# Attention, mish MoE and Sinkhorn experts: row sums turned as they are, and the sign of early weights made on GpSimd

## Chip, cores and metric

One Trainium2 chip, one core. The metric is the device time of one execution in microseconds (us); lower is better. A span is the time from the first to the last instruction of the program in a profiled execution.

## What is computed

```python
def _attn_ref(q, k, v):
    B, H, S, D = q.shape                       # 2, 8, 1152, 64
    q_pool = q.reshape(B, H, S // 2, 2, D).mean(axis=3)
    scores = 1.0 / np.sqrt(D) * np.matmul(q_pool, k.transpose(0, 1, 3, 2))
    scores = scores - np.max(scores, axis=-1, keepdims=True)
    attn = np.exp(scores)
    attn = attn / (np.sum(attn, axis=-1, keepdims=True) + 1e-09)
    return np.matmul(attn, v)
```

The heads are joined to x (1152 x 512). Then follow a mish feed-forward, `(h * tanh(softplus(h))) @ w_out` with `h = x @ w_in` (512 to 2048 to 512), and eight relu experts (512 to 1024 to 512) whose outputs are summed with weights from a gate that eight Sinkhorn rounds normalize. `w_in` and `w_out` arrive as 64-bit floats, all else as 32-bit.

## The kernel before

Every matmul works on a high and a low half of each operand, so that three products stand for one of full precision. The stages follow one another: attention (to about 265 us), mish (to about 480), the experts (to the end).

**Attention.** Heads are worked in eight pairs, each with nine query tiles of 128 rows: step g = 9p + t is tile t of pair p. Step g issues the scores of tile g and their eviction from PSUM with the row minimum (`scores`, line 483, tile e), the transposes of tile g - 3 with their split into eth (ScalarE, line 563) and etl (VectorE, line 566), the DMA that copies e to er for the transposes (`hand_over`, line 503, on SyncE's queue), products with v whose evictions write xs (line 598), and the exponentials with row sums (`exps`, line 497). The transposes and all small turns share four PSUM buffers (tag "t"). A PSUM buffer is free again when its last reader is done.

**The row sums.** `exps` collects the sums of a pair in rs (128 x 9). In the next pair, at t = 0, `row_sums` (lines 505 to 508) adds epsilon and takes the reciprocal on VectorE. At t = 1 `turn_sums` (510 to 528) transposes rs on TensorE into the PSUM tile psr (9 x 128), VectorE copies it to rt (line 515), and two DMAs on SyncE's queue follow: at the start of the next step `out` writes rt to the DRAM tile row (line 520), and at the start of the step behind it `back` reads row into rx in three broadcasts (line 526). SyncE works its queue in order: an er copy that is issued behind one of these waits with it. GpSimd multiplies xs by rx some steps later (line 607).

**The weights.** `load_w` plans the loading of 64-bit weights with a time for each step (`plan64`, lines 136 to 192): a load of the raw tile, a scaling of the high word on GpSimd or ScalarE, a scaling of the low word on ScalarE, a shift by three bits with a mask (`shift`), the sign bit put back (`sign`), an integer add on GpSimd (`join`), and the split into halves. The planner keeps a list for each engine, and each step runs what is due. Tiles with `busy=True` are worked during attention: the four tiles of the first w_in group (due at steps 16, 25, 34 and 43) and two of w_out (52 and 60). For them the shift and the sign are cut in two halves of 128 x 256; the shift of the first half is due two steps after the scaling, the sign of the first half one step later, then the second shift and sign. For a tile due at step 16 these are steps 18 to 21, so t = 0 to 3 of pair 2. `mask` is a constant column that the shift of these tiles reads as its second tensor. The tile of tag "wt" that they write has two buffers.

Of the kernel before, what the change touches and what calls it, by code (L numbers as in the profile page):

```python
# [8 lines left out]
F32 = mybir.dt.float32  # L9
# [3 lines left out]
U32 = mybir.dt.uint32  # L13
AF = mybir.ActivationFunctionType
ALU = mybir.AluOpType
# [8 lines left out]
def pool_attention_mish_sinkhorn_kernel(  # L24
# [12 lines left out]
    nc = tc.nc  # L37
    P = 128
# [10 lines left out]
    QTL = 2 * SQ // P  # L49
# [5 lines left out]
    GF = 512  # L55
    NFC = GF // P
    EPS = 1e-9

    const = ctx.enter_context(tc.tile_pool(name="const", bufs=1))
# [6 lines left out]
    make_identity(nc, ident)  # L66
    identr = const.tile([P, P], F32R, name="identr")
    nc.vector.tensor_copy(identr, ident)
    mask = const.tile([P, 1], U32, name="mask")
    nc.vector.memset(mask, 0x7FFFFFF8)  # L70
    ones = const.tile([P, P], F32, name="ones")
    nc.vector.memset(ones, 1.0)

# [26 lines left out]
    wpools = {0: wa}  # L100
# [3 lines left out]
    def at(t, eng, f):  # L104
        queue[eng].append((t, f))
# [12 lines left out]
    def load_w(which, i, times, stage, late="pool", parts=1, busy=False):  # L118
# [17 lines left out]
        def plan64(u, t):  # L136
            box = {}

            def dma():
                raw = wraw.tile([P, 2 * GF], F32, tag="raw", name=f"raw{which}_{i}_{u}")  # L140
                nc.sync.dma_start(out=raw.bitcast(I64), in_=src[:, u, :])
                w = raw.rearrange("p (n two) -> p n two", two=2)
                box["l"], box["h"] = w[:, :, 0], w[:, :, 1]

            def scale(x):
                if x and busy:
                    nc.gpsimd.tensor_scalar(box["h"], box["h"], 2.0 ** -112, 0.0, op0=ALU.mult, op1=ALU.add)
                elif x:  # L150
                    nc.scalar.activation(box["h"], box["h"], AF.Copy, scale=2.0 ** -112)
                else:
                    nc.scalar.activation(box["l"].bitcast(I32), box["l"].bitcast(U32), AF.Copy, scale=2.0 ** -29)

            def shift(cs=slice(0, GF)):
                if "t" not in box:
                    box["t"] = wpools["t"].tile([P, GF], U32, tag="wt", name=f"wt{which}_{i}_{u}")
                h = box["h"][:, cs].bitcast(U32)
                if busy:
                    nc.vector.scalar_tensor_tensor(  # L160
                        out=box["t"][:, cs], in0=h, scalar=3, in1=mask.to_broadcast(list(h.shape)),
                        op0=ALU.logical_shift_left, op1=ALU.bitwise_and)
                else:
                    nc.vector.tensor_scalar(
                        box["t"][:, cs], h, 3, 0x7FFFFFF8, op0=ALU.logical_shift_left, op1=ALU.bitwise_and)

            def sign(cs=slice(0, GF)):
                t = box["t"][:, cs]
                nc.vector.scalar_tensor_tensor(  # L169
                    out=t, in0=box["h"][:, cs].bitcast(U32), scalar=0x80000000, in1=t,  # L170
                    op0=ALU.bitwise_and, op1=ALU.bitwise_or)

            def join():
                t = box["t"].bitcast(I32)
                nc.gpsimd.tensor_tensor(out=t, in0=t, in1=box["l"].bitcast(I32), op=ALU.add)  # L175

            ts = t if isinstance(t, tuple) else [t + j * stage for j in range(5)]
            at(ts[0] - 2.4 * stage, "dma", dma)
            at(ts[0], "pool" if busy else "act", lambda: scale(1))
            at(ts[0] + parts - 1, "act", lambda: scale(0))  # L180
            for j in range(parts):
                cs = slice(j * GF // parts, (j + 1) * GF // parts)
                at(ts[1] + 2 * j, "dve", lambda cs=cs: shift(cs))
                at(ts[1] + 2 * j + parts - 1, "dve", lambda cs=cs: sign(cs))
            at(ts[2], "pool", join)
            if busy and late == "pool":
                at(ts[3], "pool", lambda: hi(nc.gpsimd, u, box["t"].bitcast(F32)))
            else:
                at(ts[3], "act", lambda: hi(nc.scalar, u, box["t"].bitcast(F32)))
            at(ts[4], late, lambda: lo(u, box["t"].bitcast(F32)))  # L190
# [107 lines left out]
    with ExitStack() as actx:  # L298
# [25 lines left out]
        tiny = pool("tiny", 4)  # L324
        wpools["t"] = pool("wt", 2)

        eps = tiny.tile([P, 1], F32, tag="eps", name="eps", bufs=1)
        nc.vector.memset(eps, EPS)
        qz = []
        for i in range(2):  # L330
            t = z_p.tile([P, 2, 2, P], F32R, name=f"qz{i}")
# [134 lines left out]
        scS, eS, erS, rsS, rxS = {}, {}, {}, {}, {}  # L466
# [35 lines left out]
            er = erS[g] = er_p.tile([P, S], F32R, tag="er", name=f"er{g}")  # L502
            nc.sync.dma_start(out=er.bitcast(F32), in_=e)

        def row_sums(p):
            rs = rsS[p]
            nc.vector.tensor_tensor(out=rs, in0=rs, in1=eps.to_broadcast([P, QTL]), op=ALU.add)
            nc.vector.reciprocal(rs, rs)

        def turn_sums(p):  # L510

            ps = ps_t.tile([P, 4, P], F32, tag="t", name=f"psr{p}")
            nc.tensor.transpose(ps[0:QTL, 0, :], rsS.pop(p), ident)
            rt = rx_p.tile([QTL, P], F32, tag="rt", name=f"rt{p}")
            nc.vector.tensor_copy(rt, ps[0:QTL, 0, :])
            row = row_p.tile([QTL, P], F32, tag="row", name=f"row{p}")
            rx = rxS[p] = rx_p.tile([P, SQ], F32, tag="rx", name=f"rx{p}")

# [196 lines left out]
        for g in range(T0 + EARLY):  # L715
            p, t = divmod(g, QTL)
# [16 lines left out]
            else:  # L733
# [19 lines left out]
                    f()  # L753
                if g < NQ:
                    exps(g)
            if p and t == 0:
                row_sums(p - 1)
            if p and t == 1:
                turn_sums(p - 1)
            if late:  # L760
# [573 lines left out]
```

## Time and profile before

| | |
|---|---|
| median of 3 runs | 1220.34 us (1220.3 to 1220.45) |
| the profiled execution | 1223.26 us |
| its span | 1221.5 us |
| TensorE (PE) busy | 1203.7 us, 99% |
| VectorE (DVE) busy | 855.8 us, 70% |
| GpSimd (POOL) busy | 654.0 us, 54% |
| ScalarE (ACT) busy | 592.1 us, 48% |
| granted TensorE clock | full throughout |

Busy time is the union of an engine's instructions. TensorE's instructions are pipelined, and its busy time holds some waiting. Busy shares over the whole span mix stages that are limited by different engines, so views of single stretches are needed. The waits view names who waited for whom, by the event that came last. The timeline shows single instructions in order.

### The profile page before, as it was taken

The page shows a single profiled execution, that of the slowest core. Times are in us where ns is not written, and L with a number is a line of the kernel's source. Part 1 is how long each engine was busy: PE and PEld are TensorE (multiplying, and loading weights), DVE is VectorE, ACT ScalarE, POOL GpSimd, SP SyncE. Part 2 cuts the span into 40 slices and gives each one's busy share as a digit, 9 for nine tenths or more (in the row PEclk, how much of TensorE's full clock was granted, in tenths as well). Part 3 has the DMA queues.
Part 4 walks back from the last instruction along what each step waited for, and adds up shares of the span by engine and source line. Part 5 has one row for each costly group of instructions (what it writes and reads, how often), then busy time and mean ns, then how long its engine had stood idle before and what let it go on. Part 6 is the DMA issues. An engine that isn't in the chain of part 4 may idle for free.

```text
span 1221.5 us, 19362 instructions
## 1 busy us (share of the span) xinstructions
PE 1203.7 (99%) x6840; PEld 1110.4 (91%) x6840; DVE 855.8 (70%) x1598; ACT 592.1 (48%) x1354; POOL 654.0 (54%) x752
## 2 busy tenths in 40 slices
PE   8899999999999999999999999999999999999998
PEld 8899999999999999898888889999888889999887
DVE  7899999876444333787866677766866777866865
ACT  7888889877544443543332233333333233333331
POOL 7667777415444331485755566555555565555551
PEclk9999999999999999999999999999999999999999
DMA  6787787653223210011111111111011111111112
GB/s 202 265 281 263 272 264 255 232 179 120 88 71 98 74 31 30 1 52 53 32 38 45 52 48 49 52 52 52 23 40 52 53 44 52 53 52 38 37 39 78
DMA packets 51985, 116.39 MB, mean 95 GB/s; under 512 B 7977, under 2 KB 22897, under 8 KB 51889
## 3 DMA queue, kind: packets, MB, share of 16 engines
q1 hardware_dynamic: 48400, 103.36, 25.9%
q0 software_dynamic: 3488, 11.80, 3.3%
q8 instruction: 54, 0.88, 0.3%
q14 instruction: 43, 0.34, 0.1%
HBM read 66.86 MB, written 2.40 MB: 57 GB/s over the span
## 4 chain that ended last, share of the span: by engine, by line
PE 90%; DVE 5%; DMA 4%; ACT 1%; issue 1%; POOL 0%; POOLq 0%; ACTq 0%
PE po L1237 30%; PE c L1067 26%; PE ph L231 10%; PE po L806 8%; PE psS L478 4%; PE psA L581 4%; DMA er<-e 4%; PE psT L560 3%; DVE e L483 2%; DVE etl L566 1%; PE psk L410 1%; PE psw L646 0%; ACT eth L563 0%; PE pg L861 0%; PE psq L456 0%
## 5 line engine op out<-in xcount | busy, mean ns | idle before, releaser
L83 POOL TENSOR_TENSOR wslotsl<-s,wslotsh 128x256 fp32r<-128x256 f32 x180 | 132.0, 743 | 237.1 <-ACT wslotsh L76 237.1
L1245 DVE SCALAR_TENSOR_TENSOR oacc<-po,Pm,oacc 128x512 f32<-128x512 f32 (+1 forms) x217 | 161.1, 746 | 102.2 <-PE po L1237 95.8
L1237 PE MATMUL po<-wdbl,hhall 128*128 128x512 f32 (+1 forms) x543 | 214.4, 395 | 0.0
L1237 PE MATMUL po<-wdbh,hlall 128*128 128x512 f32 (+1 forms) x543 | 214.1, 394 | 0.0
L1237 PE MATMUL po<-wdbh,hhall 128*128 128x512 f32 (+1 forms) x543 | 214.0, 394 | 0.0
L1084 ACT ACTIVATE t<-c 128x384 f32<-128x384 f32 x80 | 39.3, 491 | 246.2 <-PE c L1067 246.2
L1104 ACT ACTIVATE hhall<-c 128x384 fp32r<-128x384 f32 x180 | 88.6, 492 | 127.4 <-DVE c L1100 124.7
L1237 PEld LDWEIGHTS po<-wdbh,hhall 128*128 128x128 f32 x543 | 102.1, 188 | 24.3
L1237 PEld LDWEIGHTS po<-wdbl,hhall 128*128 128x128 f32 x543 | 102.1, 188 | 23.3
L1237 PEld LDWEIGHTS po<-wdbh,hlall 128*128 128x128 f32 x543 | 102.1, 188 | 23.2
L83 POOL TENSOR_TENSOR wslotsl<-rawu,wslotsh 128x256 fp32r<-128x256 f32 x120 | 90.9, 772 | 49.8 <-ACT wslotsh L76 49.8
L483 DVE TENSOR_SCALAR_CACHE_REDUCE e<-psS 128x1152 f32<-128x1152 f32 x72 | 97.3, 1352 | 22.0 <-PE psS L478 11.7
L566 DVE TENSOR_TENSOR etl<-psT,eth 128x384 fp32r<-128x384 f32 (+1 forms) x240 | 108.0, 507 | 4.8 <-ACT eth L563 4.2
L563 ACT ACTIVATE eth<-psT 128x384 fp32r<-128x384 f32 (+1 forms) x240 | 92.8, 477 | 15.6 <-PE psT L560 15.2
L1105 DVE SCALAR_TENSOR_TENSOR hlall<-c,hhall 128x384 fp32r<-128x384 f32 x180 | 98.7, 548 | 2.1
L1067 PE MATMUL c<-x2l,wslotsh 128*128 128x384 f32 x280 | 94.3, 337 | 0.0
L1067 PE MATMUL c<-x2h,wslotsl 128*128 128x384 f32 x280 | 94.1, 336 | 0.0
L1067 PE MATMUL c<-x2h,wslotsh 128*128 128x384 f32 x280 | 93.8, 335 | 0.0
L497 ACT ACTIVATE e<-e,nm 128x1152 f32<-128x1152 f32 x70 | 89.3, 1276 | 0.1
L175 POOL TENSOR_TENSOR wt<-wt,raw 128x512 int32<-128x512 int32 x32 | 42.4, 1325 | 84.0 <-DVE wt L169 59.8
L478 PE MATMUL psS<-kT,qT 128*128 128x384 f32 x384 | 81.9, 348 | 2.8 <-DVE e L483 2.7
L76 ACT ACTIVATE wslotsh<-s 128x256 fp32r<-128x256 f32 x180 | 72.0, 411 | 24.3 <-DVE s L1033 24.3
(365 smaller groups left out, 3117.2 us busy)
## 6 DMA issues: line engine op xcount, KB each, us to landing
er<-e SPq DMA_DIRECT2D x70, 576.0 KB, 4.1
rawd<-in_moe_w_dram SPq DMA_DIRECT2D x60, 256.0 KB, 2.7
rawu<-in_moe_w_dram SPq DMA_DIRECT2D x30, 384.0 KB, 3.3
raw<-in_moe_w_in_dram SPq DMA_DIRECT2D x16, 512.0 KB, 4.3
raw<-in_moe_w_out_dram SPq DMA_DIRECT2D x16, 512.0 KB, 3.7
vraw<-in_v_dram POOLq DMA_DIRECT2D x15, 288.0 KB, 4.7
kraw<-in_k_dram POOLq DMA_DIRECT2D x13, 288.0 KB, 4.6
qT<-qT SPq DMA_DIRECT2D x28, 128.0 KB, 3.1
```

Of the source, the lines that this page charges most:

```text
L83: eng.tensor_tensor(out=lo, in0=src, in1=hi.bitcast(F32), op=ALU.subtract)
L231: nc.tensor.matmul(ps[:, 0:TH], lhsT=a, rhs=b, start=(n == 0), stop=(n == len(ops) - 1))
L478: nc.tensor.matmul(ps[:, kb, 0:TH], lhsT=a, rhs=kt[:, kb * TH:(kb + 1) * TH], start=(n == 0), stop=(n == len(ops) - 1))
L483: nc.vector.tensor_scalar(sc, ps[:, :, 0:TH], -1.0, None, op0=ALU.mult, op1=ALU.min, accum_out=nm)
L497: nc.scalar.activation(e, sc, AF.Exp, bias=nm, scale=-1.0, accum_out=rsS[p][:, t:t + 1])
L563: nc.scalar.activation(eh[:, cs, o:o + b - a], ps[:, 0:3, a:b], AF.Copy)
L566: nc.vector.tensor_tensor(out=el[:, cs, o:o + b - a], in0=ps[:, 0:3, a:b], in1=eh[:, cs, o:o + b - a].bitcast(F32), op=ALU.subtract)
L806: nc.tensor.matmul(ps[:, 0:TH], lhsT=a, rhs=b, start=(n == 0), stop=(n == len(ops) - 1))
L1067: nc.tensor.matmul(cb[c], lhsT=a_, rhs=b_, start=FIRST[n] and m == 0, stop=LAST[n] and m == len(ops) - 1, skip_group_check=True)
L1105: los.append(lambda: nc.vector.scalar_tensor_tensor(out=lo, in0=b, scalar=0.0, in1=hi.bitcast(F32), op0=ALU.max, op1=ALU.subtract))
L1237: nc.tensor.matmul(ps[:, 0:w], lhsT=a, rhs=b[:, cs], start=(n == 0), stop=(n == len(ops) - 1))
L1245: nc.vector.scalar_tensor_tensor(out=oa, in0=ps[:, 0:w], scalar=gate, in1=oa, op0=ALU.mult, op1=ALU.add)
```

## The change

The constant `mask` and the tile `eps` go. `row_sums` goes: rs is transposed as `exps` left it, and in `turn_sums` VectorE adds epsilon in place in PSUM and writes the reciprocal of the 9 x 128 block to rt. For the tiles with `busy=True` GpSimd multiplies the high word twice by 2^-112 into the tile of tag "wt" (which is taken at that moment and no longer at the shift): what is left is a zero with the sign of the weight. The shift then joins its result with that zero by an or where it masked before, and `sign` isn't planned for these tiles any more.

```diff
-    mask = const.tile([P, 1], U32, name="mask")
-    nc.vector.memset(mask, 0x7FFFFFF8)
...
             def scale(x):
                 if x and busy:
+                    box["t"] = wpools["t"].tile([P, GF], U32, tag="wt", name=f"wt{which}_{i}_{u}")
+                    nc.gpsimd.tensor_scalar(
+                        box["t"].bitcast(F32), box["h"], 2.0 ** -112, 2.0 ** -112, op0=ALU.mult, op1=ALU.mult)
                     nc.gpsimd.tensor_scalar(box["h"], box["h"], 2.0 ** -112, 0.0, op0=ALU.mult, op1=ALU.add)
...
                 if busy:
                     nc.vector.scalar_tensor_tensor(
-                        out=box["t"][:, cs], in0=h, scalar=3, in1=mask.to_broadcast(list(h.shape)),
-                        op0=ALU.logical_shift_left, op1=ALU.bitwise_and)
+                        out=box["t"][:, cs], in0=h, scalar=3, in1=box["t"][:, cs],
+                        op0=ALU.logical_shift_left, op1=ALU.bitwise_or)
...
                 at(ts[1] + 2 * j, "dve", lambda cs=cs: shift(cs))
-                at(ts[1] + 2 * j + parts - 1, "dve", lambda cs=cs: sign(cs))
+                if not busy:
+                    at(ts[1] + 2 * j + parts - 1, "dve", lambda cs=cs: sign(cs))
...
-        eps = tiny.tile([P, 1], F32, tag="eps", name="eps", bufs=1)
-        nc.vector.memset(eps, EPS)
...
-        def row_sums(p):
-            rs = rsS[p]
-            nc.vector.tensor_tensor(out=rs, in0=rs, in1=eps.to_broadcast([P, QTL]), op=ALU.add)
-            nc.vector.reciprocal(rs, rs)
-
         def turn_sums(p):
 
             ps = ps_t.tile([P, 4, P], F32, tag="t", name=f"psr{p}")
             nc.tensor.transpose(ps[0:QTL, 0, :], rsS.pop(p), ident)
             rt = rx_p.tile([QTL, P], F32, tag="rt", name=f"rt{p}")
-            nc.vector.tensor_copy(rt, ps[0:QTL, 0, :])
+            sums = ps[0:QTL, 0, :]
+            nc.vector.tensor_scalar(sums, sums, EPS, None, op0=ALU.add)
+            nc.vector.reciprocal(rt, sums)
...
-            if p and t == 0:
-                row_sums(p - 1)
             if p and t == 1:
                 turn_sums(p - 1)
```

## Rows read from the trace of the kernel before

**Rows 1.** The page, busy time, share and instructions of each engine.
```profile
PE 1203.7 (99%) x6840; PEld 1110.4 (91%) x6840; DVE 855.8 (70%) x1598; ACT 592.1 (48%) x1354; POOL 654.0 (54%) x752
```

**Rows 2.** Windows of pair 3: PE, PEld, DVE, ACT, POOL busy, clock, DMA.
```profile
100.71:112.15 11.44, 11.43 (x94) 11.06 (x92) 11.34 (x25) 10.34 (x25) 9.84 (x13) 1.00 0.81 265
...
120.00:130.00 10.00, 9.54 (x80) 9.20 (x80) 8.61 (x18) 9.29 (x24) 9.44 (x10) 1.00 0.63 233
```

**Rows 3.** Waits, whole span, and SyncE's queue: us in total, times, longest.
```profile
PE psT L560 <- DMA er<-e: 7.6, 8, 2.0
...
SPq L526 <- DMA row<-rt: 11.5, 8, 2.5
```

**Rows 4.** Timeline of VectorE, pair 3, steps 0 and 1: start us, length us.
```profile
102.00 0.72 DVE L160 SCALAR_TENSOR_TENSOR wt<-raw,mask 128x256 uint32<-128x256 uint32 x1
...
104.44 0.15 DVE L507 TENSOR_TENSOR rs<-rs,eps 128x9 f32<-128x9 f32 x1
104.62 0.21 DVE L508 RECIPROCAL rs<-rs 128x9 f32<-128x9 f32 x1
104.75 1.33 DVE L483 TENSOR_SCALAR_CACHE_REDUCE e<-psS 128x1152 f32<-128x1152 f32 x1
...
106.00 0.94 DVE L169 SCALAR_TENSOR_TENSOR wt<-raw,wt 128x256 uint32<-128x256 uint32 x1
106.87 1.47 DVE L566 TENSOR_TENSOR etl<-psT,eth 128x384 fp32r<-128x384 f32 x3
108.26 0.27 DVE L515 COPY rt<-psr 9x128 f32<-9x128 f32 x1
```

**Rows 5.** Timeline of SyncE's queue, pair 3: start us, issue time us.
```profile
108.56 0.30 SPq L520 DMA_DIRECT2D row<-rt  x1
109.16 0.48 SPq L503 DMA_DIRECT2D er<-e  x1
112.02 1.75 SPq L526 DMA_DIRECT2D rx<-row  x3
113.88 0.53 SPq L503 DMA_DIRECT2D er<-e  x1
```

**Rows 6.** Timelines of ScalarE and TensorE, pair 3: two single pieces.
```profile
105.54 1.26 ACT L563 ACTIVATE eth<-psT 128x384 fp32r<-128x384 f32 x3
...
116.40 0.93 PE L560 MATMUL psT<-identr,er 128*128 128x128 f32 x9 [0.45 <-DMA er<-e]
```

**Rows 7.** Windows of line 169 alone, step 1 of pairs 2, 4, 5, 6.
```profile
74.00:76.00 2.00, 1.26 (x1) 1.00 0.61 217
...
138.00:140.00 2.00, 1.25 (x1) 1.00 0.88 323
170.00:171.00 1.00, 0.42 (x1) 1.00 1.00 371
202.00:204.00 2.00, 0.90 (x1) 1.00 0.16 46
```

**Rows 8.** Single lines: duration ns min/median/max, first and last start us, forms.
```profile
L507 DVE TENSOR_TENSOR rs<-rs,eps x8: 147/150/592, 39.9 to 261.8; 128x9 f32<-128x9 f32 x8
...
L508 DVE RECIPROCAL rs<-rs x8: 215/216/218, 40.1 to 262.0; 128x9 f32<-128x9 f32 x8
...
L900 DVE RECIPROCAL crec<-psk x8: 191/198/208, 522.7 to 562.9; 128x8 f32<-128x8 f32 x8
...
L149 POOL TENSOR_SCALAR raw<-raw x6: 639/659/680, 61.2 to 220.7; 128x512 f32<-128x512 f32 x6
```

**Rows 9.** Timeline of GpSimd, pair 3, steps 0 and 1.
```profile
101.01 1.42 POOL L83 TENSOR_TENSOR vst<-vraw,vst 128x576 fp32r<-128x576 f32 x1
...
104.57 0.68 POOL L80 TENSOR_SCALAR qst<-qraw 128x576 fp32r<-128x576 f32 x1 [0.54 <-PE psq L456]
```

**Rows 10.** Timelines of VectorE and TensorE, pair 1, steps 1 and 2.
```profile
43.39 0.27 DVE L515 COPY rt<-psr 9x128 f32<-9x128 f32 x1
...
43.78 0.93 PE L560 MATMUL psT<-identr,er 128*128 128x128 f32 x9
```

## The prediction

> **What bounds the kernel now.** I read the page first: TensorE is busy for 99% of the span [rows 1], so a change off TensorE counts only where TensorE is held up. The edits all lie in the attention stage, so the next view is the busy time by windows: in pair 3's first three steps (100.71 to 112.15 us) VectorE is busy for 11.34 of 11.44 us, more tightly packed than ScalarE or GpSimd; later in the same pair (120 to 130 us) it is busy for 8.61 of 10 [rows 2]. VectorE therefore has no room in steps t = 0 to 2 of a pair and some after that. The waits name what TensorE then pays for: 7.6 us in eight waits of the transposes for the copy er<-e, and on the DMA-issuing queue of SyncE 11.5 us in eight waits for the row write row<-rt [rows 3]. The two belong together, which the timelines of pair 3 show. VectorE finishes rt at 108.53 [rows 4]; SyncE issues the row write at 108.56, one er copy at 109.16, and then stands until the row has landed; the three rx reads go out at 112.02, and only behind them the next er copy, at 113.88 [rows 5]. TensorE's transposes at 116.40 waited 0.45 us for such a copy [rows 6]. So the end of rt is a point on the path: what makes it later makes the er copies, and with them TensorE, later.
>
> **The change, part by part, on pair 3.** The loop turns the sums of the pair before at steps t = 0 and 1 of pairs 1 to 7, and once in the tail.
>
> Removed at t = 0: the add of epsilon (0.15) and the reciprocal over 9 columns (0.21). From the add's start at 104.44 to the next eviction at 104.75 that is 0.31 us of VectorE's queue [rows 4]. Removed at t = 1: one half of the sign work, 0.94 us in pair 3, 0.87 from its start to that of the first etl (106.00 to 106.87) [rows 4]; in pairs 2, 4, 5 and 6 it took 1.26, 1.25, 0.42 and 0.90 [rows 7]. The undisturbed time is the 0.42 of pair 5; the rest is waiting for GpSimd, see below. The other half, at t = 3, goes too, but it stands behind that step's eviction, where VectorE has room: I count it as nothing, and if that room were gone it would give back up to 0.42 a pair. Pairs 1 and the tail have no sign work; in pair 7 it falls at t = 0 and 2.
>
> How much of this reaches rt? The three etl subtractions need eth from ScalarE. The first eth started at 105.54, the three take 1.26 overlapped, so one takes about 0.5 (estimate) and the first was ready near 106.04; the first etl started at 106.87 [rows 4, 6]. So etl can come forward by at most about 0.8, however much VectorE is freed.
>
> Added at t = 1, in place of the copy rt<-psr (0.27, 9 rows by 128 columns): an add of epsilon in PSUM and a reciprocal from PSUM, both over 128 columns. The add I price as the copy, 0.27, of the same shape from the same place; between it and the reciprocal stands a semaphore of VectorE on itself (the old pair had 0.03 between its add's end at 104.59 and its reciprocal at 104.62 [rows 4]). The reciprocal over 128 columns is not in the trace. Nearest rows: 9 columns from SBUF take 0.216, against 0.150 for the add over the same 9; 8 columns from PSUM take 0.198 [rows 8]. If the surplus is a fixed price, 128 columns take (0.216 - 0.150) + 0.27 = 0.34. If it is a price per column, the surplus of 0.066 over 9 columns is 7.3 ns each, and 0.27 + 128 x 0.0073 = 1.21. Bounds 0.34 and 1.21. I take 1.2: one column more costs 18 ns between the two reciprocals, though they read different memories, and a fixed surplus leaves no reason for such a step. A gain at this place is excluded: an add of the copy's shape stands where the copy stood, and the reciprocal comes on top.
> The Trainium skill, "VectorE: DVE Perf Modes", section "First, the fixed hardware budget", says that the reciprocal is an iterative division with a repeat count of 8. No run here shows the 128 columns; as eight cycles a column of the page's 0.96 GHz that would be 1.07 us besides the fixed part (an estimate from that page), so the sum would be that of the upper bound, and it speaks against turning the sums before dividing: the same 1152 quotients lie 9 in a row before and 128 in a row after.
>
> So rt and the next eviction move by 0.27 + 0.03 + 1.2 - 0.27 = +1.24, less what etl comes forward.
>
> GpSimd: six times a second TENSOR_SCALAR, priced by the old one at 0.66 (128x512) [rows 8], 3.9 us in all. It stands ahead of the scaling of the same tile, two tiles of buffer being enough, and ahead of the k and v splits queued behind it. In pair 3 the queue runs without a gap into the vst subtraction at 101.01 to 102.43 [rows 9]. The shift that stays on VectorE reads two SBUF tensors, as before; it started at 102.00, took 0.72 and ended 0.29 behind that subtraction, where the undisturbed one ends 0.42 behind its own start [rows 4, 9]. A GpSimd queue that is 0.66 later keeps it up to 0.65 longer: that cost is my estimate for pairs 3 to 6, with nothing as the other end (pair 2's shift lies behind the subtraction). Behind it GpSimd waits 0.54 us for TensorE's psq at 104.57 [rows 9], which takes up most of the 0.66; beyond the shift I cost it at nothing, and without that wait it would be 0.66 on the k and q splits.
>
> Forward move of etl, so: pair 3: 0.31 + 0.87 - 0.65 = 0.53. Pairs 2 and 4, with 1.26 and 1.25: more than 0.8, so 0.8. Pair 5: 0.31 + 0.35 - 0.65, plus 0.44 as its old add took 0.59 instead of 0.15 [rows 8], = 0.45. Pair 6: 0.31 + 0.83 - 0.65 = 0.49. Net on rt: +0.44, +0.71, +0.44, +0.79, +0.75 for pairs 2 to 6, 3.1 us together. All are on the path by the reading above: the er copies queue behind the row write.
>
> Pairs 1 and 7 have little or no sign work at t = 1, so rt is later by most of 1.24, where VectorE has room at t = 3. There the cost comes by another way: psr lies in one of four PSUM buffers of the transposes, the third group of the next step takes the same buffer, and it is free only when rt is written. In pair 1 rt was done at 43.66 and that step's nine transposes ran 43.78 to 44.71, the third group from about 44.4 [rows 10]; rt at 44.90 holds TensorE for 0.5. I take 0.45 for each of the two, with 0 and 1.24 as the ends. In the tail the turned sums feed only GpSimd's scaling; TensorE has other matmuls by then: nothing.
>
> Sum: 3.1 + 0.9 = 4.0 us. The profiled execution took 1223.26 with a span of 1221.5; the median is 1220.34, and the difference is applied to that: 1224.3.
>
> **Rivals.** (a) The reciprocal has a fixed price, 0.34. Then rt moves by 0.27 + 0.03 + 0.34 - 0.27 = +0.37 less the forward moves: -0.43, -0.16, -0.43, -0.08, -0.12 in pairs 2 to 6, and nothing in 1 and 7: 1220.34 - 1.2 = 1219.1, not slower. It decides at a reciprocal under about 0.8 us. For it: no row has more than 9 columns. Against it: the 18 ns for one more column.
> (b) The later rt is hidden: the er copies are held by their buffers (the transposes of two steps before), not by the row write, and the PSUM buffer is free in time; 1220.3 to 1222.3. For it: er copies wait for transposes too. Against it: SyncE's er copy leaves 0.6 behind the row write and the next one right behind the rx reads [rows 5].
> (c) The forward move is worth nothing, as ScalarE's eth is pushed back with TensorE: 7 x 1.24 = 8.7, so 1229.0. For it: eth hangs on transposes that wait for VectorE. Against it: VectorE's freed time lies ahead of the added time in each pair.
> (d) The saving goes through whole and the price is (a)'s: pairs 2 to 6 free 1.50, 1.18, 1.49, 1.10 and 1.14 if GpSimd does not disturb the shift, 6.4 less 5 x 0.37: 1215.8. It needs both the cheap reciprocal and an eth that comes forward too.
>
> **How the numbers follow.** Forecast 0.57 (own range 1222.9 to 1227.0, from GpSimd's part at nothing to pairs 1 and 7 at their upper end), (a) 0.08, (b) 0.20, (c) 0.10, (d) 0.05. A measurement of this kernel can tell about 0.2%, 2.4 us, from no change. Slower: nearly all of the forecast, and (c): 0.64. Same: (a), (b) and the forecast's lower edge: 0.30. Faster: (d) and a part of (a): 0.06. The range 1219.0 to 1228.0 leaves out (d), most of (c) and little else.
>
> **What would show it.** The reciprocal at 1.1 to 1.25 us for 9x128; no add and reciprocal at t = 0; the sign rows gone from the attention stage; two GpSimd rows of 0.66 per early weight tile; the row write 0.4 to 0.8 later after the eviction of step t = 1; the waits of TensorE for er<-e longer than 7.6 us, and new ones of the transposes for VectorE's rt; the mish and expert stages the same to 0.1%. A reciprocal under 0.8, or the er waits unchanged, makes it wrong.

## The result and the profile after

The changed kernel takes 1226.38 us in the median (1225.58 to 1228.59), the kernel before, beside it, 1220.32 (1218.06 to 1220.45): a ratio of 1.0057 with a 95% interval of 1.0039 to 1.0075, some 7.0 us slower. The forecast was 1224.3, slower, with a range from 1219.0 to 1228.0.

The granted TensorE clock is full (1.00, 2.4 GHz) in the profiled executions of before and after. In some of those below it was 0.50 (1.2 GHz) for a stretch of 3.4 us: with the sign alone from 59.1 us, after TensorE had been busy for 2.3 of the 4.1 us ahead of it, with the multiplications alone from 210.2, after 2.6 of 4.2. In three sets of runs the kernel before took 2.3 to 4.9 us longer, in the median, at a mean clock of 0.998 than at 1.000.

The profiled execution took 1225.82 us. Its page, the span and the busy time of each engine, answers to [rows 1]:

```profile
span 1223.9 us, 19355 instructions
PE 1208.4 (99%) x6840; PEld 1114.5 (91%) x6840; DVE 858.0 (70%) x1576; ACT 592.1 (48%) x1354; POOL 656.4 (54%) x758
```

VectorE has 22 instructions fewer and 2.2 us more of work; GpSimd has six more and 2.4 us more. The 22 are eight on the row sums (24 gone, 16 come), twelve sign halves and the fills of two constants. TensorE's busy time grew by 4.7 us though it has the same 6840 instructions. That is the first sign of something that the prediction had not looked at.

The waits, us in total, times, longest; TensorE, then SyncE's queue, answering to [rows 3]:

```profile
PE psT L557 <- DMA er<-e: 2.8, 4, 1.0
PE psS L478 <- DVE e L483: 2.7, 4, 1.5
PE psT L557 <- DVE etl L563: 1.0, 2, 0.7
PE psq L456 <- DVE etl L563: 0.8, 2, 0.4
...
SPq L523 <- DMA row<-rt: 10.5, 7, 2.4
```

The waits for er<-e did not grow from 7.6 us, they fell to 2.8. The profiled execution of before took 1223.26, 2.9 us over the median, and its waits of this kind stand at the top of what all kernels below show (1.7 to 7.6), so this pair of profiles can't settle what attention lost. In what follows medians decide on attention, and the trace only shows how.

VectorE's timeline in pair 3, steps 0 and 1 (start us, length us), answering to [rows 4]:

```profile
102.01 0.47 DVE L595 TENSOR_TENSOR xs<-psA,avt 64x320 f32<-64x320 f32 x1
102.41 1.34 DVE L483 TENSOR_SCALAR_CACHE_REDUCE e<-psS 128x1152 f32<-128x1152 f32 x1
103.68 0.07 DVE L483 DVE_READ_ACCUMULATOR e<-psS 128x1 f32 x1
103.99 1.49 DVE L563 TENSOR_TENSOR etl<-psT,eth 128x384 fp32r<-128x384 f32 x3 [0.23 <-ACT eth L560]
105.39 0.28 DVE L511 TENSOR_SCALAR psr<-psr 9x128 f32<-9x128 f32 x1
105.70 0.94 DVE L512 RECIPROCAL rt<-psr 9x128 f32<-9x128 f32 x1
106.58 1.28 DVE L483 TENSOR_SCALAR_CACHE_REDUCE e<-psS 128x1152 f32<-128x1152 f32 x1
```

Nothing stands between xs and the eviction any more, and nothing between the eviction and etl, which now waits 0.23 us for ScalarE's eth. The add and the reciprocal over 128 columns stand where the copy stood. Single lines of the changed kernel (ns min/median/max, first and last start us):

```profile
L511 DVE TENSOR_SCALAR psr<-psr x8: 277/277/277, 41.3 to 264.1; 9x128 f32<-9x128 f32 x8
L512 DVE RECIPROCAL rt<-psr x8: 945/946/947, 41.6 to 264.4; 9x128 f32<-9x128 f32 x8
L161 DVE SCALAR_TENSOR_TENSOR wt<-raw,wt x12: 407/586/2086, 67.6 to 232.2; 128x256 uint32<-128x256 uint32 x12
L150 POOL TENSOR_SCALAR raw<-raw x6: 645/664/687, 61.0 to 220.7; 128x512 f32<-128x512 f32 x6
```

The reciprocal takes 0.946 us, the new multiplication on GpSimd as long as the old one. And one half of the shift, 0.41 us by itself, took up to 2.09.

**The stages.** Lines of matmuls by their tiles carry the first and the last start, so they give the lengths of the stages. ph begins mish, c begins the experts, the last po ends them. First the kernel before (ns min/median/max; first and last start us):

```profile
L231 PE MATMUL ph<-xh,wul x192: 334/336/420, 264.8 to 442.5; 128*128 128x384 f32 x192
L806 PE MATMUL po<-hhall,wdl x144: 334/336/338, 276.1 to 470.8; 128*128 128x384 f32 x144
L1067 PE MATMUL c<-x2h,wslotsl x280: 331/334/424, 524.1 to 1196.4; 128*128 128x384 f32 x140
L1237 PE MATMUL po<-wdbh,hhall x543: 276/393/398, 540.6 to 1217.7; 128*128 128x512 f32 x179, 128*128 128x256 f32 x2
```

Then the changed kernel:

```profile
L233 PE MATMUL ph<-xh,wul x192: 334/336/420, 263.0 to 442.6; 128*128 128x384 f32 x192
L801 PE MATMUL po<-hhall,wdl x144: 334/340/341, 274.4 to 471.2; 128*128 128x384 f32 x144
L1062 PE MATMUL c<-x2h,wslotsl x280: 334/336/424, 524.5 to 1198.7; 128*128 128x384 f32 x140
L1232 PE MATMUL po<-wdbh,hhall x543: 276/395/397, 541.0 to 1220.1; 128*128 128x512 f32 x179, 128*128 128x256 f32 x2
```

Before, mish takes 524.1 - 264.8 = 259.3 us and the experts 1217.7 - 524.1 = 693.6. After, 261.5 and 695.6. No instruction of either stage was touched, the granted clock is full in both, and yet they are 2.2 and 2.0 us longer. The median matmul of one line is 340 ns long in place of 336, that of another 336 in place of 334. From one start to the next, the 144 matmuls po<-hhall,wdl are 176.5 ns apart on average, before 173.4; most others of 384 columns moved by up to 3 ns, some by nothing. This is 4.2 of the 7.0 us.

### The profile page after: what moved, and what is told of

It is laid out like the page before. It is cut to its first block, busy times and chain, and to the rows that moved or that the text cites. A ratio compares the mean times of both kernels' runs of the same rounds, so it can differ in the third digit from the quotient of the medians.

```text
span 1223.9 us, 19355 instructions
## 1 busy us (share of the span) xinstructions
PE 1208.4 (99%) x6840; PEld 1114.5 (91%) x6840; DVE 858.0 (70%) x1576; ACT 592.1 (48%) x1354; POOL 656.4 (54%) x758
## 4 chain that ended last, share of the span: by engine, by line
PE 94%; DVE 2%; DMA 2%; ACT 1%; issue 1%; SPq 0%; POOL 0%; POOLq 0%; ACTq 0%
PE po L1232 30%; PE c L1062 26%; PE ph L233 10%; PE po L801 8%; PE psS L478 6%; PE psA L578 6%; PE psT L557 3%; DMA er<-e 2%; DVE e L483 1%; PE psk L410 1%; DVE etl L563 1%; PE psq L456 0%; PE psw L643 0%; PE pg L856 0%; ACT kT L411 0%
```

## The experiments

The source of that, as the next runs show, is where the tiles lie. The constant mask took one slot of 32 bytes a partition ahead of more than half of the others. Without it 460 of the 950 tiles lie 32 bytes lower, the activations of mish and the experts and a part of their weights among them, and 86 others 64 bytes lower; 404 stay where they were, among them the weights wdh and wdl of mish and wdbh and wdbl of the experts. So the change has three parts: the sums, the sign, and the removal of the constants as a move of other tiles. The theory after the first reading was that the code costs what attention lost and the move costs the 4.2 us; the rival was that the code has a late effect on the long stages (through what is still queued when mish begins). Ratios below are against the kernel before on the same chip, with 95% intervals; 0.001 is 1.22 us. Where it changes a reading, the medians of the executions at a mean clock of 1.000 alone are given too.

**The move alone.** Against the kernel before:

```diff
-    mask = const.tile([P, 1], U32, name="mask")
-    nc.vector.memset(mask, 0x7FFFFFF8)
...
+        mask = tiny.tile([P, 1], U32, tag="mask", name="mask", bufs=1)
+        nc.vector.memset(mask, 0x7FFFFFF8)
```

> The kernel before with one edit: the column mask lies among the small tiles of the attention stage instead of ahead of ones, so that every instruction is the old one and only the tiles that lay behind mask (x, weights, e, er, rx, xs, later acc, hidden) lie 32 bytes lower in SBUF, as they do in the changed kernel. Chain theory (the time comes from rt being later in pairs 1 to 7): no change, 1220.3 within 1. Placement theory (the matmuls of mish and of the experts, which no edit touches, were slower in the changed kernel's trace by 2.0 us each because of where their operands lie): mish and experts together +4 us, po matmuls of mish at about 176.5 ns from start to start where they had 173.3, and 1222 to 1226 in all.

Measured: 1221.8 us, ratio 1.0019 [1.0007, 1.003], +2.3 us, with every instruction as before. Mish took 261.6 and the experts 696.6 us, 5.3 more than before, with po<-hhall,wdl again 176.5 ns apart. So the move makes the matmul stages slower by itself. Its attention must then be some 3 us shorter (2.3 - 5.3): the move has a second, opposite effect there.

**The code alone.** Against the changed kernel, the constants filled again and read by nothing, so that each tile lies where it lay:

```diff
+    mask = const.tile([P, 1], U32, name="mask")
+    nc.vector.memset(mask, 0x7FFFFFF8)
...
+        eps = tiny.tile([P, 1], F32, tag="eps", name="eps", bufs=1)
+        nc.vector.memset(eps, EPS)
```

> The changed kernel with both dropped tiles (mask and eps) kept, filled and unread, so that all other tiles lie where they lay before. Chain theory: the loss stays, about 1224 to 1226. Placement theory: mish and experts as before; what is left is what the two edits do in the attention stage, between 1219 and 1222, with the reciprocal at 0.946 us instead of the forecast 1.2.

Measured: 1224.22 us, ratio 1.0036 [1.0022, 1.0049], +4.4 us; mish 259.4 and experts 693.7 as before. All of it lies in attention. The code's 4.4 and the move's 2.3 make 6.7 of the 7.0 us: the two parts add up. In six kernels below that keep the matmul operands of mish and the experts at the old addresses the two stages together took 952.9 to 953.1 us, in the sums alone 953.7; before took 952.9.

**The sums alone**, at the old addresses (the edits of row_sums and turn_sums, with eps kept):

```diff
-            if p and t == 0:
-                row_sums(p - 1)
...
-            nc.vector.tensor_copy(rt, ps[0:QTL, 0, :])
+            sums = ps[0:QTL, 0, :]
+            nc.vector.tensor_scalar(sums, sums, EPS, None, op0=ALU.add)
+            nc.vector.reciprocal(rt, sums)
```

> The kernel before with the row sums' edit alone (no add and reciprocal at step 0; add in PSUM and reciprocal over 128 columns at step 1); all tiles lie as before. Without the sign's relief rt is later in each of pairs 1 to 7 by 0.28 + 0.03 + 0.95 - 0.27 = 0.99 less up to 0.31. Chain theory: +4.8 to +6.9 us, so 1225 to 1227. Placement theory says nothing on it beyond that mish and experts take their old time; if the queue has more slack than the chain reading says, 1221 to 1223.

Measured: 1224.64 us, ratio 1.0041 [1.0026, 1.0056], +5.0 us. TensorE's waits for VectorE, of this kernel's waits and of its timeline in pair 3 (the scores of step 3):

```profile
PE psS L478 <- DVE e L483: 4.2, 9, 1.5
...
108.27 1.32 PE L478 MATMUL psS<-kT,qT 128*128 128x384 f32 x6 [0.27 <-DVE e L483]
```

Before they were 2.7 us in 4 waits. The scores of step 3 wait 0.27 to 0.32 us in each of pairs 2 to 6, because the eviction that frees their PSUM buffer stands behind the reciprocal. The transposes wait once a pair too, 0.05 to 0.08 us, but these waits end 0.05 behind the end of ScalarE's copy to kT, which the trace names as their releaser; none of TensorE's waits is put down to rt, which frees psr's buffer. rt ends 4.73 us behind the start of the eviction of step 1 (mean of pairs 2 to 6: 5.30, 4.50, 4.50, 4.56, 4.80), before 3.80 (4.11, 3.78, 4.10, 3.26, 3.75).

**The same time on VectorE, but rt on time.** Against the kernel before, a reciprocal that nothing reads, behind the copy:

```diff
             nc.vector.tensor_copy(rt, ps[0:QTL, 0, :])
+            nc.vector.reciprocal(ps[0:QTL, 0, :], ps[0:QTL, 0, :])
```

> The kernel before with one instruction more in each of the eight turns: behind the copy to rt, VectorE takes the reciprocal of psr in place, 9x128, 0.95 us, which nothing reads. rt is on time; VectorE's next eviction is 0.9 us later, and the PSUM buffer of psr comes free that much later. Chain theory: 0 to 1.5 us, so 1219.7 to 1221.2. Queue theory (what counts is the eviction behind it and the buffer): 4 to 5 us as with the row sums' edit, 1223.5 to 1225.

Measured: 1222.66 us, ratio 1.0015 [1.0, 1.003], +1.8 us. Both lines over psr (ns):

```profile
L515 DVE COPY rt<-psr x8: 269/269/279, 41.4 to 265.5; 9x128 f32<-9x128 f32 x8
L516 DVE RECIPROCAL psr<-psr x8: 944/944/944, 41.6 to 265.7; 9x128 f32<-9x128 f32 x8
```

rt ends 3.54 us behind the eviction's start, no later than before (3.80). Over all executions the 0.94 us more on VectorE, with the buffer held as long, cost 1.8 of the 5.0 us. But 11 of the 23 executions of before that stand beside it had a mean clock under 1.000, and only 2 of this kernel's 12. At 1.000 alone the medians are 1222.57 and 1218.88, +3.7, and those of the sums alone 1224.47 and 1219.67, +4.8. So most of what the sums cost comes without a later rt. What is left, 1 to 3 us, would go with the later rt or with the old add and reciprocal that the sums edit takes out; with intervals of about 1.5 us on either side it is not shown.

**The row write a step later**, without and with the sums edit, for pairs 1 to 7: does rt's lateness act by the row write that SyncE's queue waits for?

```diff
-            first.append(out)
+            first.append(out if p == NPAIR - 1 else lambda: first.append(out))
```

> The kernel before with the row write and the rx reads of pairs 1 to 7 issued one step later each, so that SyncE never stands for rt ahead of an er copy at step 2. Chain theory (er copies are late because they queue behind the row write and the rx reads): up to 2 us gained, 1217.7 to 1219. If the er copies are held by their buffers or by their landing: 1219.7 within 1.

> The row sums' edit alone with the row write and the rx reads of pairs 1 to 7 one step later each. It took 1224.6 with the old issue times. Chain theory: the loss is in rt's way to the er copies, which this takes away; 1220 to 1221.5 is left. If the loss is VectorE's queue (the next eviction 1 us later, and TensorE's scores behind it) or the PSUM buffer of psr, it stays: 1223.5 to 1225.

Measured: 1233.79 (1.0108 [1.0084, 1.0132]) and 1233.74 (1.0107 [1.0081, 1.0132]). Both lie far outside what was expected. With the later issue the sums edit costs nothing, as it would if rt's lateness were taken up by the slack that the later issue makes; but in a kernel that is 13 us longer other waits may hide it too, and these runs do not tell the two apart. The delay itself costs the 13 us. Eleven of the twelve executions had a mean clock under 1.000 (0.993 to 0.998), yet the one at 1.000 took 1232.6. (In the profiled execution of the first kernel the experts took 696.2 us, with no tile moved: there the clock stood at 0.50 for 3.4 us from 562.9.) In the first of the two kernels SyncE's queue and GpSimd show:

```profile
SPq L526 <- DMA row<-rt: 5.4, 4, 2.0
...
POOL xs L607 <- DMA rx<-row: 26.4, 4, 8.6
```

The waits of SyncE for the row fell from 11.5 us in 8 [rows 3] to 5.4 in 4, and the kernel became slower: those waits were not time that could be won by standing elsewhere. GpSimd now waits for rx in four places, 26.4 us together, all within attention, where before there was one there, of 7.3 (and 22.7 us in the tail); it works its queue in order, and a shift on VectorE took up to 3.18 us there (0.98 before). How the 13 us divide among these is open.

**The sign alone**, at the old addresses (the three edits of load_w with mask kept):

```diff
+                    box["t"] = wpools["t"].tile([P, GF], U32, tag="wt", name=f"wt{which}_{i}_{u}")
+                    nc.gpsimd.tensor_scalar(
+                        box["t"].bitcast(F32), box["h"], 2.0 ** -112, 2.0 ** -112, op0=ALU.mult, op1=ALU.mult)
...
-                at(ts[1] + 2 * j + parts - 1, "dve", lambda cs=cs: sign(cs))
+                if not busy:
+                    at(ts[1] + 2 * j + parts - 1, "dve", lambda cs=cs: sign(cs))
```

> The kernel before with the sign's edit alone (12 sign halves of VectorE gone, six GpSimd multiplications more); mask stays where it was, unread, and all tiles lie as before. Chain theory: rt comes up to 0.8 us sooner in pairs 2 to 6, so 1217 to 1220. If the longer GpSimd queue holds the shifts (up to 2.09 us in the changed kernel's trace), the gain is lost: 1220 to 1222.

Measured: 1224.26 us, ratio 1.003 [1.0017, 1.0042], +3.7 us. This is outside both expectations. rt did come sooner by the 0.8 that the chain theory had: it ends 3.00 us behind the start of the eviction of step 1 (mean of pairs 2 to 6), before 3.80. An edit that takes at least twelve times 0.42 us off the packed VectorE, and brings rt forward, makes the kernel slower.

**GpSimd's multiplication without the gain** (the added tile and multiplication of the diff above; the mask and the sign halves stay):

```diff
+                    box["t"] = wpools["t"].tile([P, GF], U32, tag="wt", name=f"wt{which}_{i}_{u}")
+                    nc.gpsimd.tensor_scalar(
+                        box["t"].bitcast(F32), box["h"], 2.0 ** -112, 2.0 ** -112, op0=ALU.mult, op1=ALU.mult)
```

> The kernel before with the sign's six GpSimd multiplications added, but the old masked shift and the 12 sign halves kept (the product is overwritten by the shift). If the 0.66 us that they push GpSimd's queue back is the cost of the sign's edit (VectorE's two-tensor operations then meet GpSimd's subtractions): 1222 to 1224. If not: 1219.7 to 1220.5.

Measured: 1228.8 us, ratio 1.0072 [1.0051, 1.0093], +8.8 us for 3.9 us of added GpSimd work, above what either theory had. Five of its six executions were at a mean clock of 0.997 to 0.999; the one at 1.000 took 1228.93, against 1218.88 for before at 1.000, so the clock does not explain it.

**The gain without GpSimd's multiplication** (the early weights lose their signs here; the sign halves are left out and nothing stands for them):

```diff
-                at(ts[1] + 2 * j + parts - 1, "dve", lambda cs=cs: sign(cs))
+                if not busy:
+                    at(ts[1] + 2 * j + parts - 1, "dve", lambda cs=cs: sign(cs))
```

> The kernel before without the 12 sign halves of the early weight tiles and with nothing in their place: the early weights lose their signs, so this times the removal alone. If removal is a gain as the chain theory has it: 1217 to 1219. If VectorE's freed time only moves the meetings with GpSimd to the next two-tensor operation: 1219 to 1222.

Measured: 1220.44 us, ratio 0.9993 [0.9972, 1.0014] (at a clock of 1.000 alone 1220.45 against 1218.88): what the sign edit takes away is worth nothing that can be measured, what it adds costs 8.8 us by itself. In this kernel rt ends 2.93 us behind the start of the eviction of step 1, 0.87 sooner than before, with no GpSimd work added, and nothing is gained. That speaks against the chain theory. How the multiplications cost so much, the timelines of pair 4 show. In the kernel before, VectorE and under it GpSimd (start us, length us):

```profile
134.34 0.42 DVE L160 SCALAR_TENSOR_TENSOR wt<-raw,mask 128x256 uint32<-128x256 uint32 x1
...
132.90 1.43 POOL L83 TENSOR_TENSOR vst<-vraw,vst 128x576 fp32r<-128x576 f32 x1
134.62 0.59 POOL L347 DMA_DIRECT2D vraw<-in_v_dram  x1 [0.30 <-POOL vst L83]
```

GpSimd's subtraction ends at 134.33, the shift starts at 134.34 and takes its 0.42. In the kernel with the multiplications alone:

```profile
131.02 1.75 DVE L163 SCALAR_TENSOR_TENSOR wt<-raw,mask 128x256 uint32<-128x256 uint32 x1
134.49 1.67 DVE L510 TENSOR_TENSOR rs<-rs,eps 128x9 f32<-128x9 f32 x1
...
130.42 0.67 POOL L393 TENSOR_SCALAR qraw<-qraw 128x576 f32<-128x576 f32 x1
131.06 1.43 POOL L83 TENSOR_TENSOR vst<-vraw,vst 128x576 fp32r<-128x576 f32 x1
...
134.69 1.44 POOL L83 TENSOR_TENSOR kst<-kraw,kst 128x576 fp32r<-128x576 f32 x1
```

The shift starts at 131.02, while GpSimd's scaling of q still runs (to 131.09). It does not come in between that and the subtraction that follows at 131.06; it ends at 132.77, 0.28 behind the subtraction's end at 132.49. The add of epsilon over nine columns, 0.15 us by itself, starts at 134.49 and takes 1.67, to the end of the kst subtraction. And in the changed kernel itself:

```profile
130.93 2.09 DVE L161 SCALAR_TENSOR_TENSOR wt<-raw,wt 128x256 uint32<-128x256 uint32 x1
...
130.66 0.67 POOL L390 TENSOR_SCALAR qraw<-qraw 128x576 f32<-128x576 f32 x1
131.29 1.42 POOL L81 TENSOR_TENSOR vst<-vraw,vst 128x576 fp32r<-128x576 f32 x1
```

The shift ends at 133.02, about 0.3 behind the subtraction's 132.71. Between 60 and 262 us of the five kernels in the table below, nearly every shift or sign half that took over 0.47 us ended 0.28 to 0.29 us behind the end of a GpSimd instruction, mostly a vst or kst subtraction, and every longer add ended within 0.04 of such an end or, where it was short, of that of the scaling ahead of it. GpSimd's instructions keep their lengths; it is VectorE that waits. Summed over 60 to 262 us (time above 0.41 for the shift, 0.42 for the sign, 0.15 for the add; the last column is what TensorE's waits for VectorE come to there):

| kernel | shift | sign | add of epsilon | sum, us | TensorE for VectorE, us |
|---|---|---|---|---|---|
| before | 1.30 | 2.69 | 0.45 | 4.44 | 0.4 |
| multiplications alone | 7.62 | 3.21 | 4.82 | 15.65 | 6.2 |
| the sign alone | 4.76 | none | 2.12 | 6.88 | 1.9 |
| without the sign halves | 5.07 | none | 2.09 | 7.16 | 2.8 |
| changed kernel | 5.71 | none | none | 5.71 | 2.5 |

The multiplications alone add 11.2 us of such waiting, on a VectorE that has no room there (11.34 of 11.44 us in [rows 2]), and the kernel became 8.8 us longer. TensorE then waits for VectorE (60 to 262 us; before, of these, only once for e, 0.3):

```profile
PE psS L481 <- DVE e L486: 2.9, 4, 0.9
PE psr L516 <- DVE rs L511: 1.1, 3, 0.4
PE psk L413 <- DVE etl L569: 0.8, 3, 0.3
PE psq L459 <- DVE etl L569: 0.8, 2, 0.4
```

GpSimd itself is not what limits there: in that kernel it is idle for 70.8 of the 202 us, and the waits of other engines that are put down to it come to 0.4 us. Without the sign halves the waiting went up too, though GpSimd did nothing new: the shift and the add now meet the long subtractions which the sign halves met before. These sums do not give the times by themselves, though: the sign alone and the kernel without sign halves have about the same, 6.88 and 7.16, and differ by 3.8 us in their medians, with the six multiplications as the only difference (they ran on different chips; against before the difference is 4.6, with wide intervals). What else the multiplications cost there stays open. So freed time on VectorE is partly taken back by the next two-tensor instruction, since the two queues stand differently to one another.

**Where the tiles lie, three more times.** First only the attention tiles 32 bytes higher, all else at its address:

```diff
+        pad = pool("pad", 1).tile([P, 1], F32, tag="pad", name="pad")
+        nc.vector.memset(pad, 0.0)
```

> The kernel before with one 32-byte tile placed ahead of e, so that the attention stage's tiles on that side (e, er, the transposed scores, k and v tiles, rt, rx, xs) lie 32 bytes higher, on the same offset within 64 as in the changed kernel, while x, the weights and the later hidden and acc tiles stay; every other instruction is the old one. Placement theory, as the run with mask moved showed it: its 4.3 us of slower matmuls in mish and experts don't appear, and if the attention stage gained 2 us there by where its tiles lie, that stays: about 1217.7. If that gain came from x or the raw weight tiles, or was chance: 1219.7.

Then what follows the constants on their side 32 bytes higher, and 64 bytes higher:

```diff
+    pad = const.tile([P, 1], U32, name="pad")
+    nc.vector.memset(pad, 0)
```

> The kernel before with one unread 32-byte column ahead of ones, so that everything that mask's removal moved 32 bytes down lies 32 bytes up instead. If the offset within 64 bytes decides, mish and experts take the 261.5 and 696 us of the two kernels with the lower tiles, and the whole is near 1221.8. If it is the exact place, they stay at 259.4 and 693.9, and the whole is at 1219.7.

The second has `[P, 16]` in place of `[P, 1]`.

> Every instruction as before, plus one memset; one unread column of 64 bytes a partition ahead of `ones` puts everything behind it 64 bytes higher, so each tile has the same place within 64 bytes as before. Where the slow matmuls of the changed kernel come from the place of the tiles within 64 bytes: the mish matmuls po<-hhall,wdl start 173.4 ns apart as before and the time is 1220.3, ratio 0.998 to 1.002. Where any move away from the old addresses costs, or a place within more than 64 bytes counts: 176 ns or more as in the kernels that move by 32 bytes, and 1222 to 1227, ratio 1.002 to 1.006.

Its lines of matmuls, to be held against those of before above:

```profile
L233 PE MATMUL ph<-xh,wul x192: 334/336/420, 259.6 to 438.8; 128*128 128x384 f32 x192
L808 PE MATMUL po<-hhall,wdl x144: 336/337/343, 271.0 to 467.5; 128*128 128x384 f32 x144
L1069 PE MATMUL c<-x2h,wslotsl x280: 332/334/424, 520.8 to 1195.6; 128*128 128x384 f32 x140
L1239 PE MATMUL po<-wdbh,hhall x543: 278/392/404, 537.3 to 1217.0; 128*128 128x512 f32 x179, 128*128 128x256 f32 x2
```

Neither expectation of the move by 32 bytes came out; the move by 64 fell where any move costs. In the moves that reach mish and the experts 405 of the tiles stay (490 in the run with mask moved), wdh, wdl, wdbh and wdbl among them, so the operands of one matmul also lie at another distance from each other. A move of all tiles together was not tried. All kernels that only move tiles, with the stage lengths read in the same way, and two kinds of matmul by the mean from start to start:

| tiles | median us | ratio | mish us | experts us | po<-hhall,wdl ns | c<-x1h,wslotsh ns |
|---|---|---|---|---|---|---|
| before | 1220.3 | 1 | 259.3 | 693.6 | 173.4 | 173.3 |
| attention 32 higher | 1218.78 | 0.9987 [0.9971, 1.0002] | 259.3 | 693.6 | 173.2 | 173.4 |
| from the constants on 32 lower | 1221.8 | 1.0019 [1.0007, 1.003] | 261.6 | 696.6 | 176.5 | 173.4 |
| the same 32 higher | 1226.25 | 1.006 [1.0041, 1.0078] | 261.7 | 698.2 | 177.0 | 176.7 |
| the same 64 higher | 1222.89 | 1.002 [1.0007, 1.0034] | 261.2 | 696.2 | 175.4 | 175.0 |

The place within 64 bytes is not the rule: 64 bytes higher is slow too, and the two moves by 32 bytes, which agree within 64, differ by 1.5 us in the experts and in c<-x1h,wslotsh by 3.3 ns. Every move of the matmul operands that was tried, the changed kernel's among them, costs 4.2 to 7 us in mish and experts, and which lines pay for it differs. The attention stage, by what is left of the whole, becomes shorter under two of the three moves (2.3 - 5.3 and 2.4 - 4.5) and stays under the third (7.3 - 7.0); with only its own tiles moved it is 1.6 us shorter, which the interval does not separate from nothing (0.6 at a clock of 1.000 alone). What about an address, or about two operands' distance, does this stays open.

## Why the prediction was right, and where its steps were not

The sign, the median within the range and the size for the code (4.0 forecast, 4.4 measured at unmoved addresses) came out. The sum behind them did not: two terms were mis-sized, one had the wrong sign, one is not in the trace, and a part of the change was not priced at all. That the sizes agree is in large part luck.

**The end of rt as a point on the path.** All 4.0 us of the sum rest on a later rt, 3.1 of them by way of the er copies. The runs do not bear that out. In the kernel without the sign halves rt ends 0.87 us sooner in the mean of pairs 2 to 6, and the time stays (1220.44); with the sign alone it ends 0.80 sooner, and the kernel is 3.7 us slower. The same time on VectorE with rt on time costs 3.7 of the sums' 4.8 at a clock of 1.000. What the trace of the sums alone shows in its place is VectorE's queue: the next eviction comes later, and the scores of step 3 wait for it by 0.3 a pair. In the changed kernel even that wait is gone (2.7 us in 4 waits, as before). The waits that TensorE has for VectorE there (2.5 us where before had 0.4) are most of them for etl, and they do not make up 4.4.

**The stages behind attention, "the same to 0.1%".** The step that failed outright. Mish and experts went from 952.9 to 957.1 us, 0.44%. The prediction listed what the change does to instructions and left out that it removes a constant, and with it moves the operands of every matmul behind it. Nothing in the profile of before could have given the size; that the diff deletes a tile ahead of all others could be seen.

**The reciprocal, 1.2 between bounds of 0.34 and 1.21.** It took 0.946. Against the 0.198 for 8 columns from PSUM [rows 8] that is 0.748 for 120 columns, 6.2 ns each, where the estimate had 7.3 on top of the copy. The choice of a price for each column was right, and with it rival (a) fell: it decides below 0.8. By the Trainium skill, "VectorE: DVE Perf Modes", section "First, the fixed hardware budget", the repeat count of 8 read as eight cycles a column gave, as an estimate, 1.07 us besides the fixed part; the row lies below that, so that reading does not hold. The add and the gap, 0.27 and 0.03, came as forecast (0.277; 105.67 to 105.70).

**The forward move of etl, at most about 0.8.** In the changed kernel rt ends 4.11 us behind the start of the eviction of step 1 (mean of pairs 2 to 6: 4.26, 4.24, 3.93, 3.93, 4.20), before 3.80: +0.31, where the mark was 0.4 to 0.8. That eviction itself stands 0.31 closer to what is ahead of it without the old add and reciprocal, so the net on rt is about nothing, not the 0.44 to 0.79 that the sum used. The cheaper reciprocal accounts for 0.25 of that. The rest is that etl came forward by more: in pair 4 from 2.44 (136.79 to 139.23) to 1.27 (134.73 to 136.00) behind the eviction's start, 1.17 where 0.8 was the limit. In pair 3 ScalarE's eth did hold it, by 0.23.

**GpSimd's part, 0.65 on the shift.** The mechanism was seen, a shift that ends behind GpSimd's subtraction; its size was bounded by the delay of GpSimd's queue, and that was the error. A VectorE instruction that starts under the GpSimd instruction just ahead of a subtraction waits for all of the subtraction too, so a shift in time of 0.66 can turn a wait of nothing into one of 1.67 (0.42 to 2.09 in pair 4). The rule of the Trainium skill, "SBUF — State Buffer", section "Who interferes with whom", is that a VectorE instruction with two SBUF inputs contends with a GpSimd instruction that reads SBUF; the shared pair of ports is an exclusive lock, which for VectorE's two-port modes the page gives to whoever issues first, for the whole instruction. The traces agree with that order for these two-input instructions too (0.42 us became 2.09), and add that the waiting one can be passed by a second GpSimd instruction queued without a gap. The prediction had the whole sign edit as a gain, against the sums' loss; alone it is a loss of 3.7 us, as its added half costs 8.8 and its removed half returns nothing.

**Pairs 1 and 7, 0.45 each by the PSUM buffer.** This wait is not in the trace. Behind the reciprocal's start TensorE's transposes wait 0.08 us once a pair, but these waits end 0.1 to 0.3 us ahead of rt's end, and 0.05 behind ScalarE's copy to kT. What the sums alone cost TensorE directly is the wait of the scores of step 3, which the prediction did not name.

**The waits for er<-e, to be longer than 7.6.** They were 2.8 us. The mark was a poor one: it rested on one execution, and the waits do not go with the times: 1.7 us in the sums alone (+5.0), 3.0 with only the attention tiles moved (-1.6). The prediction named these waits, unchanged, as a sign of being wrong; a rise is seen in none of the kernels.

**The rivals.** (b), that a later rt is hidden, has the wrong time for the code (4.4, where it allowed 2.0), but its mechanism is not refuted. (c), that the freed time is worth nothing, fits the run without the sign halves; it gave 8.7 for the code. The parts alone make 5.0 + 3.7 = 8.7, together 4.4, so the two edits help each other, as the prediction had it, though neither is a gain. A likely reason, not tested by itself: the sign half that goes at step 1 gives the reciprocal its place, and the old add of epsilon, which in the sign-only kernel waited 2.12 us for GpSimd, is gone. How the 4.4 us divide between the reciprocal and the shift's waits when both are there was not settled.

## What to carry to other kernels

Look at what a change does to the addresses before costing its instructions: a deleted constant moved 460 tiles by 32 bytes, and the matmul stages became 0.4% slower; an experiment that keeps a dummy in its place separates the two. Before work is moved from VectorE to GpSimd, list the VectorE instructions with two SBUF tensors next to it: each can wait for a whole GpSimd instruction, however short it is itself, and on a packed VectorE such waits can cost more than the moved work's own time (8.8 us for 3.9 here). Before a later tile is called costly, a run that makes it earlier, or that spends the same engine time without making it later, tells whether it is on the path; and two kernels are compared at the same granted clock. A reciprocal wants few columns and many partitions: the same 1152 quotients took 0.22 us as 128x9 from SBUF and 0.95 as 9x128 from PSUM.

## What the runs showed of the hardware that was not expected

- The same matmuls at full granted clock run 173.4 or 176.5 ns apart on average (384 columns, po<-hhall,wdl), by nothing but the place of their tiles, of which some moved and others stayed; five placements gave 952.9 to 959.9 us for mish and experts.
- A VectorE instruction with two SBUF tensors ends mostly 0.28 to 0.29 us (128x256) or within 0.04 (128x9) behind the GpSimd instruction that it meets, and was prolonged by up to 1.67 us in the changed kernel.
- A reciprocal of 9x128 from PSUM takes 0.946 us, 6.2 ns for each column above eight; the add over the same block 0.277.
- Six multiplications on GpSimd, 0.66 us each, made the kernel 8.8 us longer.
